# Batch 1's first transform in front of the fixed rows' read, and x laid out one tile to a transfer

## The chip, the core and the metric

The kernel runs on one core of a Trainium2 chip. The metric is device time in microseconds from start to end of one execution on that core; lower is better. Five engines work side by side, each through its own list of instructions in order: TensorE (PE, with its weight loads as PEld), VectorE (DVE), ScalarE (ACT), GpSimd (POOL) and SyncE (SP). All but TensorE and VectorE also issue transfers (DMAs) here, and these run on 16 DMA engines.

## The reference

A spectral filter over each of 8 batches, and behind it a mixture of 8 experts in which each row goes to one expert only.

```python
batch, seq, dim = (8, 2496, 256)            # float32
X = np.fft.rfft(x, axis=1)
F = (filt_r + 1j * filt_i)[None, :, :]
y = np.fft.irfft(X * F, n=seq, axis=1)      # -> 19968 rows of 256

xn = y / (norm(y) + 1e-06);  en = expert_emb / (norm(expert_emb) + 1e-06)
logits = xn @ en.T / tau
expert_idx = np.argmax(logits, axis=1)
gate_w = softmax(logits)[arange, expert_idx]
for e in range(8):                          # w1[e]: 256 x 1024, w2[e]: 1024 x 256
    mask = expert_idx == e
    h = np.maximum(y[mask] @ w1[e], 0.0)
    out[mask] = gate_w[mask, None] * (h @ w2[e])
```

## The kernel before, in words

**The transform.** 2496 = 64 × 39, so each batch's transform is done as matrix products: a first one over 39 points (`conv_s1`, tiles s_g_t: 11 tiles of 117 x 2 rows of x for batch g), a second one over 64 points with the filter in its middle (`conv_s2`, 10 steps of s and sa), and an inverse over 39 (`conv_sb`, tiles y). Between the stages the rows are written to DRAM (SD, ZD) and read back in another order (tiles a, and f for both the filter and ZD). Tiles of x are read into four buffers called `in`, which the tiles a share.

**The experts.** Rows of y get a norm, logits and the routing (`route`, L705), in chunks: batch 0 is routed as 12 and 10 half tiles. GpSimd then scatters each half tile to its expert's region of a table in DRAM (XS, `scatter_rows` L794). Work on the experts is cut into slots. A slot reads 128 or 256 rows of one expert back, transposed (`read_pair` L892, `read_rows` L882; tiles xTf and metaf for batch 0), multiplies with the expert's first matrix in four parts (ph_j_0 to ph_j_3, L973), takes the relu on ScalarE and VectorE (h_j_p, L981 and L982) and multiplies with the second matrix (po, L998). The first eight slots, one for each expert, are of 128 rows each and need only the first chunk of batch 0's rows. They are called the fixed rows here.

**The weights.** Each expert's matrices come as float32 (L264) and are made into a scaled float16 high half (ScalarE, L324) and a low half (VectorE, L331). Their scale comes from a product of the matrix with itself (gram, 16 small products, L286), its diagonal's greatest value (dg and wmax, L291 and L292) and a sum of that (L296).

**The order.** In the head, 82 steps long, the order on TensorE, VectorE, ScalarE and SyncE is that of the code (L1166 to L1177). In each step `head()` issues one piece of the transforms, `weights(n)` what is due of the weights, and from step 66 (SLOTS) a part of a slot follows. From step 35 on `head()` walks through batch 0's inverse (`back`, with its routing) and through batch 1's first transform (`ahead`) side by side: step n of `back` is head step 35 + n.

```python
        for n, w in enumerate(back):
            if n == XNEXT - 35:
                next(ahead)
            ...
            yield w
            if n >= SIDE and n not in PAUSE:
                next(ahead, 0)
        yield from ahead
```

At XNEXT the first x tiles of batch 1 are asked for. From step SIDE of `back` one of its 11 tiles is transformed in each step, save in the steps of PAUSE. Of `weights(n)`, WLOADS says in which steps the 16 halves of the weights are loaded, WPREP what of their preparation is done in a step (g: product, d: diagonal, p and q: scale, k: high half, l: low half, each with expert and part), and at step FIRST_ROWS = 64 the first two experts' fixed rows are read. WLATE does the rest of the preparation, by the count of slot parts.

Transfers issued by SyncE and ScalarE count up one of eight counters, DMAHW0 to DMAHW7, which are given to them in turn; a transfer waits until the one before it on its counter has landed.

Behind the head the order is worked out by a scheduler, from costs that are the same in both kernels.

Of the kernel before, what the change touches and what calls it, by code (L numbers as in the profile page):

```python
# [13 lines left out]
F32 = mybir.dt.float32  # L14
# [10 lines left out]
P = 128  # L25
NA, NB39 = 64, 39
S = NA * NB39
NK2 = 20
A3 = 3
TOK = A3 * NB39  # L30
NAG = (NA + A3 - 1) // A3
D = 256
# [8 lines left out]
XYB, INB, CYB = 6, 4, 7  # L41
# [4 lines left out]
G_S1, G_SB, G_S2, G_SA = 2, 3, 4, 3  # L46
DLAG = 2
MID = 8
XNEXT = 45
WLOADS = (38, 40, 42, 44, 46, 48, 50, 52, 54, 56, 58, 60, 62, 64, 78, 79)  # L50
WPREP = {43: "g00", 44: "g01", 46: "d0", 47: "p0", 48: "q0", 49: "k00 g10", 50: "l00 k01", 51: "l01 k02 g11",
# [5 lines left out]
WLATE = {16: "l53 q6 g70", 17: "k60 g71", 18: "l60 k61 d7", 19: "l61 k62 p7", 20: "l62 k63 q7", 21: "l63 k70",  # L57
         22: "l70 k71", 23: "l71 k72", 24: "l72 k73", 25: "l73"}
SIDE, PAUSE = 24, (28, 29, 30)
CLEAR, FIRST_ROWS = 39, 64  # L60
SLOTS, HEAD = 66, 82
WARM = {-1: 8, 12: 26, 35: 22, 40: 6}
# [12 lines left out]
def moe_spectral_kernel(  # L75
# [287 lines left out]
    def widths(g):  # L363

        return NAG * GROUPS[g][0] // 2, NK2 * GROUPS[g][0] // 2


    def whole(g, ap, t, rows, full):

        if GROUPS[g][0] == 2:  # L370
            k = rows(t)
            return [(slice(0, 2), k, ap(t, k, False))]
        if rows(2 * t) == rows(2 * t + 1):
            return [(slice(0, 2), full, ap(t, full, False))]
        return [(slice(j, j + 1), rows(2 * t + j), ap(2 * t + j, rows(2 * t + j), True)) for j in range(2)]

    def x_at(g):
        def at(t, k, half):
            if GROUPS[g][0] == 2:
                return x[first[g]:first[g] + 2, t * TOK:t * TOK + k].rearrange("b p c -> p b c")  # L380
            if half:
                return x[first[g], t * TOK:t * TOK + k].unsqueeze(1)
            return x[first[g], t * 2 * TOK:(t + 1) * 2 * TOK].rearrange("(j p) c -> p j c", j=2)
        return at

    def buf_at(g, buf):
        def at(t, k, half):
            if GROUPS[g][0] == 2:
# [9 lines left out]
    def load(q, g, pool, tag, t, ap, rows, full):  # L398
        it = pool.tile([P, 2, D], F32, tag=tag, name=f"{tag}{g}_{t}")
        got = []  # L400
        for h, k, m in whole(g, ap, t, rows, full):
            q.dma_start(it[:k, h], m)  # L402
            got.append((h, it[:k, h].rearrange("p j c -> p (j c)")))
        return got

    cons = {"c1": c1_sb, "c2": c2_sb, "m1": m1_sb, "csb": csb_sb}

# [41 lines left out]
    def conv_s1(g):  # L449

        NTL, _ = widths(g)
        if g == G_S1:
            cons["c1"] = parts_of(cons["c1"], "c1")
        xin = {t: load(nc.gpsimd if g > 1 else nc.sync, g, cin, "in", t, x_at(g), tokens, TOK) for t in range(INB - 1)}
        if g == 1:
            yield 0
        for t in range(NTL):
            if t + INB - 1 < NTL:
                xin[t + INB - 1] = load(nc.gpsimd if g > 1 else nc.sync, g, cin, "in", t + INB - 1, x_at(g), tokens, TOK)
            if g >= G_S1:  # L460
                u = t
                xin[u] = split(*pair(f"xp{g}_{u}"), xin[u])
            pool, tag = (ps_h, "h") if g == 1 and t < 4 else (ps_c, "c")
            pt = pool.tile([P, 2, D], F32, tag=tag, name=f"s1_{g}_{t}")
            for h, xt in xin.pop(t):
                product(pt[:, h].rearrange("p j c -> p (j c)"), cons["c1"], xt)
            st = cst.tile([P, 2, D], F32, tag="st", name=f"s{g}_{t}")
            nc.scalar.copy(st, pt)  # L468
            for h, k, m in whole(g, buf_at(g, SD[g]), t, freqs, 120):
                (nc.scalar if g == 1 else nc.sync).dma_start(m, st[:k, h])  # L470
            yield W_S1
# [233 lines left out]
    def route(g, out_rows, t0, n, rows, ssq, rr, lp, sg=None):  # L705
# [39 lines left out]
        oh = big("oh", F16)  # L745
        v.tensor_tensor(out=oh, in0=w8.unsqueeze(1).to_broadcast([P, nt, E]), in1=bc(mv), op=ALU.is_equal)
        yield 1
        if not g and t0 + n // 2 < widths(g)[0]:
            yield 1

        nc.scalar.activation(ex, l, AF.Exp)
        state["routed"] += 1
        base = state["base"]
# [310 lines left out]
    def head():  # L1064
        yield from conv_s1(0)
        yield from conv_s2(0)
        back, ahead = conv_sb(0), conv_s1(1)
# [3 lines that stand above are left out]
            if state["routed"] and not run["fixed"]:  # L1071
                run["fixed"] = True
                enqueue(0, "fixed")
            yield w
            if n >= SIDE and n not in PAUSE:
                next(ahead, 0)
        yield from ahead

# [177 lines left out]
```

## Time and profile before

| | before |
|---|---|
| median of 3 runs | 1359.09 us (1356.71, 1364.03, 1359.09) |
| the profiled execution | 1363.88 us, of it 1361.6 in the span |
| mean granted clock of TensorE | 0.963 |
| TensorE busy | 1246.3 us (92%), weight loads 980.6 (72%) |
| VectorE, ScalarE, GpSimd busy | 69%, 56%, 38% |
| moved by DMA | 240.64 MB |
| loads of x (L402) | 60 of 234 KB each on GpSimd and 20 on SyncE, with the two halves of the last tile beside them |

The profile is of one execution. A window's row gives each engine's busy time in a stretch, with its count of instructions. A row of the timeline gives the start, the duration, the engine, the line, the operation with output and inputs, and in brackets the idle time just ahead with what ended it. SPq, ACTq and POOLq are transfers being issued by SyncE, ScalarE and GpSimd. PEclk is the clock that TensorE was granted, as a share of full speed.

### The profile page before, as it was taken

Reading aid. Unit: us, or ns where it says so; the run is one execution under the profiler, and the core shown is the slowest. Engines: PE = TensorE matmul, PEld = TensorE weight load, DVE = VectorE, ACT = ScalarE, POOL = GpSimd, SP = SyncE. Lnnn points to the kernel's source line nnn. Section 1 sums busy time; section 2 is a strip of 40 time slices with the busy share of each in tenths; the row PEclk is TensorE's granted clock in tenths of the full one; section 3 lists DMA queues with packets and bytes.
Section 4 is the critical chain, followed back from the end, with each engine's and each line's share of the span. In section 5 each row is a group of like instructions: output and inputs, shape, how many; then the busy total and the mean of one; then the engine's idle time right before and its main releaser. Section 6 shows DMA issues by size and latency. Waiting matters only on the chain.

```text
span 1361.6 us, 36510 instructions
## 1 busy us (share of the span) xinstructions
PE 1246.3 (92%) x11027; PEld 980.6 (72%) x11027; DVE 940.1 (69%) x3078; ACT 761.5 (56%) x1760; POOL 513.2 (38%) x575
## 2 busy tenths in 40 slices
PE   7865799959997989999999999999999999999998
PEld 2333575635665768777788788878887788889887
DVE  1456686765676758887879787878786786444664
ACT  2174545744673668567747794768465843333343
POOL 0004413174337424752365347443642165211212
PEclk9987899979998989999999999999999899999999
DMA  7898787877987677777778797878774544231221
GB/s 225 270 324 282 207 246 205 187 218 229 198 176 214 195 185 176 199 226 178 174 181 242 185 200 184 228 188 195 169 201 139 129 119 106 52 60 40 48 48 41
DMA packets 275758, 240.64 MB, mean 177 GB/s; under 512 B 167845, under 2 KB 217902, under 8 KB 273777
## 3 DMA queue, kind: packets, MB, share of 16 engines
q1 hardware_dynamic: 246409, 177.71, 51.4%
q0 software_dynamic: 25280, 57.51, 14.5%
q10 hardware_dynamic: 3880, 3.03, 0.7%
q8 instruction: 104, 1.70, 0.6%
q14 instruction: 85, 0.70, 0.2%
HBM read 121.68 MB, written 85.57 MB: 152 GB/s over the span
## 4 chain that ended last, share of the span: by engine, by line
PE 64%; DMA 13%; issue 5%; DVE 4%; ACT 3%; POOL 1%; SPq 0%; DVEq 0%; POOLq 0%; ACTq 0%
PE ph L973 25%; PE po L998 24%; PE s L447 4%; DMA yT<-rows 4%; PE y L447 3%; DMA a<-SD 2%; PE sa L447 2%; PE s L442 2%; DMA f<-ZD 2%; DMA XS<-rows,ixi 1%; PE y L442 1%; PE tp L596 1%; PE lp L613 1%; DVE wp L957 1%; DMA SD<-s 1%
## 5 line engine op out<-in xcount | busy, mean ns | idle before, releaser
L998 PE MATMUL po<-W,h 128*128 (+1 forms) x3824 | 494.3, 273 | 0.0
L973 PE MATMUL ph<-xT,wp 128*128 128x256 f16 (+2 forms) x4224 | 476.2, 260 | 11.0 <-DMA xT<-XS 5.2
L973 PEld LDWEIGHTS <-wp 128*128 128x128 f16 x4224 | 360.6, 99 | 90.2 <-issue 40.5
L998 PEld LDWEIGHTS <-h 128*128 128x128 f16 x3824 | 361.2, 98 | 70.2 <-issue 27.6
L981 ACT ACTIVATE h<-ph 128x512 f16<-128x512 f32 (+2 forms) x384 | 202.0, 528 | 249.0 <-PE ph L973 194.7
L1013 POOL DMA_INDIRECT out_dram<-o,meta x153 | 159.4, 1042 | 309.8 <-ACT o L1012 231.0
L982 DVE SCALAR_TENSOR_TENSOR h<-ph,h 128x512 f16<-128x512 f32 (+2 forms) x384 | 227.3, 592 | 57.3 <-ACT h L981 55.4
L957 DVE COPY wp<-W 128x1024 f16 x352 | 168.0, 478 | 113.1 <-PE ph L973 108.5
L796 POOL DMA_INDIRECT XS<-rows,ixi x176 | 185.3, 1053 | 126.3 <-issue 53.7
L539 POOL TENSOR_TENSOR yy<-yy,xs 128x512 f32<-128x512 f32 x60 | 80.8, 1350 | 107.5 <-DVE xs L502 74.8
L402 POOL DMA_DIRECT2D in<-in_x x72 | 56.4, 784 | 161.2 <-DVE xp L416 44.2
L500 DVE TENSOR_TENSOR yy<-s,f 128x256 f32<-128x256 f32 x160 | 61.4, 418 | 63.6 <-ACT xs L532 25.8
L671 ACT ACTIVATE rows<-y 128x256 f16<-128x256 f32 x176 | 67.3, 398 | 35.1 <-PE y L442 33.3
L638 DVE SCALAR_TENSOR_TENSOR rows<-y,rr,rows 128x256 f16<-128x256 f32 x176 | 76.6, 477 | 14.7 <-ACT rows L635 13.4
L1012 ACT ACTIVATE o<-po,meta 128x256 f32<-128x256 f32 x148 | 64.2, 480 | 27.8 <-PE po L998 27.5
L635 ACT ACTIVATE rows<-y,rr 128x256 f16<-128x256 f32 x176 | 75.7, 499 | 6.3 <-DVE rr L676 5.1
L561 ACT COPY z<-sa 128x512 f32<-128x512 f32 x80 | 46.8, 585 | 50.0 <-PE sa L558 43.7
L468 ACT COPY s<-s 128x512 f32<-128x512 f32 x88 | 52.7, 600 | 30.8 <-PE s L442 14.5
L415 ACT CAST yp<-yy 128x512 fp32r<-128x512 f32 x50 | 30.9, 619 | 62.5 <-POOL yy L539 62.3
L598 ACT COPY yT<-tp 128x512 f16<-128x512 f16 x99 | 59.0, 610 | 7.0 <-PE tp L596 5.9
L447 PE MATMUL s<-xp,c1h 117*128 117x512 f32 (+1 forms) x144 | 60.8, 429 | 0.6 <-DVE sg L217 0.6
L613 PEld LDWEIGHTS <-yT 128*128 128x128 f16 x704 | 32.7, 97 | 37.2 <-DMA yT<-rows 18.2
(208 smaller groups left out, 1679.5 us busy)
## 6 DMA issues: line engine op xcount, KB each, us to landing
f<-in_filt SPq DMA_DIRECT2D x160, 256.0 KB
a<-SD SPq DMA_DIRECT2D x80, 256.0 KB
ZD<-z SPq DMA_DIRECT2D x80, 256.0 KB
f<-ZD SPq DMA_DIRECT2D x80, 240.0 KB
SD<-s SPq DMA_DIRECT2D x70, 240.0 KB
W<-in_w SPq DMA_DIRECT2D x14, 1024.0 KB
in<-in_x POOLq DMA_DIRECT2D x60, 234.0 KB
in<-in_x SPq DMA_DIRECT2D x20, 234.0 KB
```

The source lines that it names most:

```text
L447: nc.tensor.matmul(out_, w[:k], b, start=(n == 0), stop=(n == 2))
L539: nc.gpsimd.tensor_tensor(out=yy, in0=yy, in1=xs, op=ALU.add)
L635: nc.scalar.activation(rows[:, i, 0:D], y[:, i], AF.Copy, scale=rr[:, u:u + 1])
L638: nc.vector.scalar_tensor_tensor(out=rows[:, i, D:2 * D], in0=y[:, i], scalar=rr[:, u:u + 1], in1=rows[:, i, 0:D], op0=ALU.mult, op1=ALU.s ...
L671: nc.scalar.activation(rows[:, i, D:2 * D], y[:, i], AF.Square, accum_out=ssq[:, u + i:u + i + 1])
L796: i = nc.gpsimd.indirect_dma_start(out=XS, out_offset=bass.IndirectOffsetOnAxis(ap=ix, axis=0), in_=src, in_offset=None)
L957: last["dve"] = nc.vector.tensor_copy(wp, src)
L973: last["pe"] = nc.tensor.matmul(ph[:, fi, :size], wp[:, k * 2 + wh, fi * P:(fi + 1) * P], xT[:, xh * 2 + k, :size], start=(c == 0), stop=( ...
L981: last["act"] = nc.scalar.activation(h[:, 0, :, :size], ph[:, :, :size], AF.Relu)
L982: last["lo"] = nc.vector.scalar_tensor_tensor(out=h[:, 1, :, :size], in0=ph[:, :, :size], scalar=0.0, in1=h[:, 0, :, :size], op0=ALU.max, ...
L998: nc.tensor.matmul(self.po[:, s], h, self.Wp[:, off + wh * 1024:off + wh * 1024 + D], start=(fp == 0 and fi == 0 and c == 0), stop=(fp == ...
L1013: i = nc.gpsimd.indirect_dma_start(out=out, out_offset=bass.IndirectOffsetOnAxis(ap=self.meta[:n, s, 0:1].bitcast(I32), axis=0), in_=o, in ...
```

## The change

It does three things.

1. The x tiles of batch 1 are asked for two steps sooner (XNEXT 45 to 43), and the transform of them starts at step 18 of `back` instead of 24 and is not paused: head steps 53 to 63, in place of 59 to 62 and 66 to 72. All of it stands ahead of FIRST_ROWS = 64. In `route`, one of the two pauses behind the first chunk's `oh` goes.
2. The last two weight loads of the first run come a step sooner, and WPREP and WLATE are laid out anew: most pieces one to three steps later, the last at count 27 in place of 25.
3. x is laid out on the way in as 8 × 11 × 117 × 2 × 256, padded with zeros, so that a tile is one transfer in which each partition gets one run of 2048 bytes. Before, a tile was two runs of 1024 bytes per partition, and the last one, of 117 and 39 rows, came in two transfers. Now it is full, too.

```diff
@@ -46,17 +46,17 @@
 G_S1, G_SB, G_S2, G_SA = 2, 3, 4, 3
 DLAG = 2
 MID = 8
-XNEXT = 45
-WLOADS = (38, 40, 42, 44, 46, 48, 50, 52, 54, 56, 58, 60, 62, 64, 78, 79)
-WPREP = {43: "g00", 44: "g01", 46: "d0", 47: "p0", 48: "q0", 49: "k00 g10", 50: "l00 k01", 51: "l01 k02 g11",
...
-WLATE = {16: "l53 q6 g70", 17: "k60 g71", 18: "l60 k61 d7", 19: "l61 k62 p7", 20: "l62 k63 q7", 21: "l63 k70",
...
-SIDE, PAUSE = 24, (28, 29, 30)
+XNEXT = 43
+WLOADS = (38, 40, 42, 44, 46, 48, 50, 52, 54, 56, 58, 60, 61, 63, 78, 79)
+WPREP = {43: "g00", 44: "g01", 46: "d0", 48: "p0", 49: "q0 g10", 50: "k00", 51: "l00 k01 g11", 52: "d1 l01 k02",
...
+WLATE = {16: "l52 k53 p6", 17: "l53 q6 g70", 18: "k60 g71", 19: "d7 l60 k61", 20: "l61 k62", 21: "l62 k63 p7",
...
+SIDE = 18
 CLEAR, FIRST_ROWS = 39, 64
 SLOTS, HEAD = 66, 82
 WARM = {-1: 8, 12: 26, 35: 22, 40: 6}
@@ -374,15 +374,6 @@
             return [(slice(0, 2), full, ap(t, full, False))]
         return [(slice(j, j + 1), rows(2 * t + j), ap(2 * t + j, rows(2 * t + j), True)) for j in range(2)]
 
-    def x_at(g):
-        def at(t, k, half):
-            if GROUPS[g][0] == 2:
-                return x[first[g]:first[g] + 2, t * TOK:t * TOK + k].rearrange("b p c -> p b c")
-            if half:
-                return x[first[g], t * TOK:t * TOK + k].unsqueeze(1)
-            return x[first[g], t * 2 * TOK:(t + 1) * 2 * TOK].rearrange("(j p) c -> p j c", j=2)
-        return at
-
     def buf_at(g, buf):
         def at(t, k, half):
             if GROUPS[g][0] == 2:
@@ -402,6 +393,12 @@
             q.dma_start(it[:k, h], m)
             got.append((h, it[:k, h].rearrange("p j c -> p (j c)")))
         return got
+
+    def load_x(g, t):
+
+        it = cin.tile([P, 2, D], F32, tag="in", name=f"in{g}_{t}")
+        (nc.gpsimd if g > 1 else nc.sync).dma_start(it[:TOK], x[first[g], t])
+        return [(h, it[:k, h].rearrange("p j c -> p (j c)")) for h, k, _ in whole(g, lambda *a: None, t, tokens, TOK)]
 
     cons = {"c1": c1_sb, "c2": c2_sb, "m1": m1_sb, "csb": csb_sb}
 
@@ -451,12 +448,12 @@
         NTL, _ = widths(g)
         if g == G_S1:
             cons["c1"] = parts_of(cons["c1"], "c1")
-        xin = {t: load(nc.gpsimd if g > 1 else nc.sync, g, cin, "in", t, x_at(g), tokens, TOK) for t in range(INB - 1)}
+        xin = {t: load_x(g, t) for t in range(INB - 1)}
         if g == 1:
             yield 0
         for t in range(NTL):
             if t + INB - 1 < NTL:
-                xin[t + INB - 1] = load(nc.gpsimd if g > 1 else nc.sync, g, cin, "in", t + INB - 1, x_at(g), tokens, TOK)
+                xin[t + INB - 1] = load_x(g, t + INB - 1)
             if g >= G_S1:
                 u = t
                 xin[u] = split(*pair(f"xp{g}_{u}"), xin[u])
@@ -745,9 +742,6 @@
         oh = big("oh", F16)
         v.tensor_tensor(out=oh, in0=w8.unsqueeze(1).to_broadcast([P, nt, E]), in1=bc(mv), op=ALU.is_equal)
         yield 1
-        if not g and t0 + n // 2 < widths(g)[0]:
-            yield 1
-
         nc.scalar.activation(ex, l, AF.Exp)
         state["routed"] += 1
         base = state["base"]
@@ -1072,7 +1066,7 @@
                 run["fixed"] = True
                 enqueue(0, "fixed")
             yield w
-            if n >= SIDE and n not in PAUSE:
+            if n >= SIDE:
                 next(ahead, 0)
         yield from ahead
 
@@ -1227,8 +1221,10 @@
     fr = filt_r[src.T].transpose(0, 1, 2)
     fi = filt_i[src.T].transpose(0, 1, 2)
     filt = np.stack([np.concatenate([fr, fr], 1), np.concatenate([fi, fi], 1)], 2)
+    xp = np.zeros((nb, 2 * ((NAG + 1) // 2) * TOK, D), x.dtype)
+    xp[:, :S] = x[:, perm]
     arrays = {
-        "x": x[:, perm],
+        "x": xp.reshape(nb, -1, 2, TOK, D).transpose(0, 1, 3, 2, 4),
         "filt": filt,
         "sgn": sgn,
         "c1": c1,
```

SyncE around the fixed rows' first read. `in_k` is the tile k of x, W half an expert's matrices, XS the table of rows, SD what the first transform writes. Before:

```order
L264 DMA W<-in_w 128x2048 [waits DMAHW0_49]
L402 DMA in_6_1325<-in_x 117x2x256 [waits DMAHW2_49,PE_49]
L884 DMA_TRANSPOSE xTf_1350<-XS 128x4x128 [waits DMAHW3_49,DMASW3_49]
L885 DMA metaf_1351<-XS 128x2 [waits DMAHW4_49]
L884 DMA_TRANSPOSE xTf_1350<-XS 128x4x128 [waits DMAHW5_49]
L885 DMA metaf_1354<-XS 128x2 [waits DMAHW7_49]
L264 DMA W<-in_w 128x2048 [waits DMAHW0_49]
L402 DMA in_7_1418<-in_x 117x2x256 [waits DMAHW1_49,PE_49]
L884 DMA_TRANSPOSE xTf_1460<-XS 128x4x128 [waits DMAHW2_49]
L885 DMA metaf_1461<-XS 128x2 [waits DMAHW4_49]
```

Now:

```order
L264 DMA W<-in_w 128x2048 [waits DMAHW6_49]
L400 DMA in_10_1286<-in_x 117x512 [waits DMAHW0_49,PE_49]
L264 DMA W<-in_w 128x2048 [waits DMAHW1_49]
L264 DMA W<-in_w 128x2048 [waits DMAHW3_49]
L878 DMA_TRANSPOSE xTf_1393<-XS 128x4x128 [waits DMAHW4_49,DMASW3_49]
L879 DMA metaf_1394<-XS 128x2 [waits DMAHW5_49]
L878 DMA_TRANSPOSE xTf_1393<-XS 128x4x128 [waits DMAHW7_49]
L879 DMA metaf_1397<-XS 128x2 [waits DMAHW0_49]
L878 DMA_TRANSPOSE xTf_1477<-XS 128x4x128 [waits DMAHW1_49]
L879 DMA metaf_1478<-XS 128x2 [waits DMAHW3_49]
```

Before, the reads of the first two experts' rows have a load of W and of in_7 between them, and in_8 to in_10 come later still. Now all of x and three loads of W stand ahead, and the four reads follow each other. The third read is given DMAHW1 and the columns behind it DMAHW3.

ScalarE at the same place: s_k are tiles of batch 1's first transform, ex_6 and ixi_6 belong to the routing of batch 0's second chunk, h_0_0 to the first fixed slot. Before:

```order
L468 COPY s_3_1329<-s_1_3_1327 128x512 [waits PE_49]
L470 DMA SD_209<-s_3_1329 120x2x256 [waits DMAHW3_49,Activation_49]
L751 ACTIVATE ex_6_1344<-l_6_1332 128x80 [waits DVE_49]
L776 CAST ixi_6_1387<-ix_6_1385 128x10 [waits DVE_49]
L324 ACTIVATE W<-W,wsc 128x1024 [waits DMAHW2_49]
L324 ACTIVATE W<-W,wsc 128x1024
L981 ACTIVATE h_0_0_1415<-ph_0_0_1402 128x2x128 [waits PE_49]
```

Now:

```order
L465 COPY s_9_1364<-s_1_9_1362 128x512 [waits PE_49]
L467 DMA SD_209<-s_9_1364 120x2x256 [waits DMAHW6_49,Activation_49]
L465 COPY s_10_1378<-s_1_10_1375 128x512 [waits PE_49]
L467 DMA SD_209<-s_10_1378 120x256 [waits DMAHW1_49,Activation_49]
L467 DMA SD_209<-s_10_1378 40x256 [waits DMAHW3_49]
L745 ACTIVATE ex_6_1387<-l_6_1367 128x80 [waits DVE_49]
L770 CAST ixi_6_1432<-ix_6_1430 128x10 [waits DVE_49]
L324 ACTIVATE W<-W,wsc 128x1024
L975 ACTIVATE h_0_0_1455<-ph_0_0_1442 128x2x128 [waits PE_49]
```

Before, s_3 is written out ahead of ex_6, and s_4 follows behind h_0_0. Now s_9 and s_10 stand there. The first write of s_10 waits on DMAHW1, the second on DMAHW3; both are given their counter behind the reads.

TensorE where batch 1's second transform (s_1_0) begins; gram and ph belong to the weights and the slots. Before:

```order
L286 LDWEIGHTS wraw_3_1915
L286 MATMUL gram_2054<-wraw_3_1915 128x128
L442 MATMUL s_1_0_2133<-a_0_2085,c_sb 128x512
L442 MATMUL s_1_1_2158<-a_1_2087,c_sb 128x512
L296 LDWEIGHTS one_142
L296 MATMUL gram_1823<-wmax,one_142 128x2
L973 LDWEIGHTS W
L973 MATMUL ph_3_3_1978<-xTf_1460,W 128x128
```

Now:

```order
L286 LDWEIGHTS W
L286 MATMUL gram_1495<-W 128x128
L439 MATMUL s_1_0_2114<-a_0_2059,c_sb 128x512
L439 MATMUL s_1_1_2139<-a_1_2061,c_sb 128x512
L967 LDWEIGHTS W
L967 MATMUL ph_0_3_1556<-xTf_1393,W 128x128
```

Before, s_1_0 stands ahead of ph_3_3, the last part of the fourth slot. Now it stands ahead of ph_0_3, the last part of the first one.

## Rows read from the trace of the kernel before

**Rows 1.** Windows: busy times by stage, granted clock and DMA share.

```profile
core 0: us, PE busy (x) PEld busy (x) DVE busy (x) ACT busy (x) POOL busy (x), PEclk, DMA share, GB/s
97.80:131.90 34.10, 22.19 (x186) 14.64 (x187) 23.55 (x82) 18.30 (x39) 15.23 (x13) 0.70 0.90 303
131.90:140.90 9.00, 0.04 (x2) 0.04 (x2) 2.93 (x16) 1.47 (x4) 0.17 (x1) 0.50 0.56 159
140.90:148.10 7.20, 7.20 (x65) 5.41 (x65) 4.17 (x11) 3.03 (x6) 5.72 (x5) 0.71 1.18 291
148.10:227.70 79.60, 74.47 (x686) 53.14 (x684) 60.12 (x159) 44.78 (x78) 18.50 (x18) 1.00 0.71 215
...
238.30:312.90 74.60, 55.88 (x488) 37.05 (x489) 49.10 (x248) 42.80 (x124) 33.66 (x41) 0.84 0.79 204
```

**Rows 2.** Waits of TensorE, 0 to 260: total, times, longest.

```profile
PE gram L296 <- DVE wmax L292: 14.8, 4, 9.0
...
PE s L442 <- DMA in<-in_x: 4.9, 5, 1.8
```

**Rows 3.** Timeline of TensorE around the hole.

```profile
140.86 0.16 PE L296 MATMUL gram<-wmax,one 128*128 128x2 bf16 x1 [8.97 <-DVE wmax L292]
140.88 1.44 PE L973 MATMUL ph<-xTf,W 128*128 128x128 f16 x12
...
146.08 1.08 PE L442 MATMUL s<-in,c_sb 117*128 117x512 f32 x2
146.99 1.08 PE L286 MATMUL gram<-W 128*128 128x128 bf16 x16
147.91 0.83 PE L973 MATMUL ph<-xTf,W 128*128 128x128 f16 x12
```

**Rows 4.** Timeline of the other engines, routing and first read.

```profile
112.11 1.88 POOL L796 DMA_INDIRECT XS<-rows,ixi  x1 [19.47 <-DVE done L878]
...
128.80 1.79 POOL L796 DMA_INDIRECT XS<-rows,ixi  x1 [0.30 <-issue]
...
134.11 1.31 SPq L884 DMA_TRANSPOSE xTf<-XS  x1
...
136.92 0.32 ACTq L470 DMA_DIRECT2D SD<-s  x1
137.29 0.27 ACT L751 ACTIVATE ex<-l 128x80 f32<-128x80 f32 x1 [8.48 <-DMA xTf<-XS]
...
137.59 0.24 DVE L763 TENSOR_REDUCE se<-ex 128x10 f32<-128x80 f32 x1 [6.38 <-ACT ex L751]
...
139.70 0.20 ACT L776 CAST ixi<-ix 128x10 int32<-128x10 f32 x1 [2.14 <-DVE ix L773]
...
142.77 0.42 DVE L982 SCALAR_TENSOR_TENSOR h<-ph,h 128x256 f16<-128x256 f32 x1 [0.51 <-ACT h L981]
142.86 3.04 SPq L489 DMA_DIRECT2D f<-in_filt  x4
```

**Rows 5.** Chain that ended last: start, length, step.

```profile
128.80 5.30 DMA XS<-rows,ixi
134.11 2.74 DMA xTf<-XS
...
172.84 7.39 DMA a<-SD
...
197.86 2.44 DMA a<-SD
```

**Rows 6.** DMA queue at 12 to 16, then 30 to 35.

```profile
q1 hardware_dynamic: 1169, 1.13, 90.4%
...
q1 hardware_dynamic: 842, 1.54, 94.0%
```

**Rows 7.** Timeline of TensorE, batch 1's first inverse row.

```profile
238.25 2.07 PE L442 MATMUL y<-f,csb_sb 120*128 120x512 f32 x2 [3.39 <-DMA f<-ZD]
```

**Rows 8.** Costly lines 0 to 260: the low halves on VectorE.

```profile
L331 DVE SCALAR_TENSOR_TENSOR W<-W,wsc 128x1024 f16<-128x1024 f32 x27 | 34.3, 1274 | 3.7 <-ACT W L324 3.7
```

More of the change, by code (lines that the diff above doesn't have):

```diff
@@ L48 @@
 MID = 8
-XNEXT = 45
-WLOADS = (38, 40, 42, 44, 46, 48, 50, 52, 54, 56, 58, 60, 62, 64, 78, 79)
-WPREP = {43: "g00", 44: "g01", 46: "d0", 47: "p0", 48: "q0", 49: "k00 g10", 50: "l00 k01", 51: "l01 k02 g11",
[5 rows of a table removed]
-WLATE = {16: "l53 q6 g70", 17: "k60 g71", 18: "l60 k61 d7", 19: "l61 k62 p7", 20: "l62 k63 q7", 21: "l63 k70",
-         22: "l70 k71", 23: "l71 k72", 24: "l72 k73", 25: "l73"}
-SIDE, PAUSE = 24, (28, 29, 30)
+XNEXT = 43
+WLOADS = (38, 40, 42, 44, 46, 48, 50, 52, 54, 56, 58, 60, 61, 63, 78, 79)
+WPREP = {43: "g00", 44: "g01", 46: "d0", 48: "p0", 49: "q0 g10", 50: "k00", 51: "l00 k01 g11", 52: "d1 l01 k02",
[5 rows of a table added]
+WLATE = {16: "l52 k53 p6", 17: "l53 q6 g70", 18: "k60 g71", 19: "d7 l60 k61", 20: "l61 k62", 21: "l62 k63 p7",
+         22: "l63 q7", 23: "k70", 24: "l70 k71", 25: "l71 k72", 26: "l72 k73", 27: "l73"}
+SIDE = 18
 CLEAR, FIRST_ROWS = 39, 64
```

10 rows, old and new, of the table WPREP are left out of this document.

## The prediction

> **What bounds the kernel now.** I read the profile from the front to the place where the two orders become alike again: first the windows, then TensorE's waits, the timeline around the widest hole, the chain that ended last, and the DMA queue. The windows [rows 1] show where TensorE has room: 22.19 busy of 34.1 us while batch 0 is routed (97.8 to 131.9), 0.04 of 9.0 just behind it (131.9 to 140.9), then 74.47 of 79.6 (94%) up to the end of batch 1's middle stages, and 55.88 of 74.6 in the stage where batch 1 is routed. Behind 312.9 TensorE is 92 to 100% busy by the page's slices, so a lead won before then reaches the end unless a wait swallows it. The stage from 238 to 312.9 is such a candidate: routing, scatters and the read follow each other there. But its order on TensorE is the same in both kernels from batch 1's first inverse row [rows 7], so I take it as a fixed length behind that row. The question is how much sooner the row at 238.25 comes.
>
> The largest single wait is 9.0 us for a norm of the weights on VectorE, L292 [rows 2]. The timeline [rows 3, 4] shows that the norm is only the last of a chain. The last scatter of the first chunk is issued at 128.80, takes 5.30 to land [rows 5], and at 134.11 SyncE issues the first transposing read, which lands 2.74 later, 136.85. ScalarE's write of s_3 is issued at 136.92, and `ex` behind it on ScalarE starts at 137.29: both had waited for the read, since that write waits for the counter (DMAHW3) that the read counts up. Then VectorE's seven small steps (137.59 to 139.70), the norm, and at 140.86 TensorE runs again.
>
> **The change part by part.**
> *First transform moved in front of the read.* Seven tiles of x come to stand in front of the hole. A tile takes 0.91 us on TensorE at full clock (146.08 to 146.99 [rows 3]), 6.4 in all; the room in 97.8 to 131.9 is 11.9 us [rows 1], so they hide there if x is there in time. Two of the seven stood between ph_0_0 and ph_0_2 before, five behind ph_0_2. What follows ph_0_2 at 147.91 is a full stretch, so there the five save 5 × 0.91 = 4.55. A norm's product (16 matmuls, 146.99 to 147.91: 0.92) goes in front too. About 0.5 of slot work moves the other way, behind the second transform (an estimate: half a product of the kind at 147.91). Net 4.1 us less between ph_0_2 and the end of the second transform.
>
> *The start of that stretch.* The read is the fixed point; call its issue T. T follows the last scatter. The pause of one step that is taken out of the routing lets the scatters begin sooner than 112.11 [rows 4], but 4 x tiles, one W and all the SD writes now share the DMA queues with them. If the scatters, 1.5 us apart on average now ((128.80 − 112.11)/11), came back to back at about 1.3, T would be near 131.5; if the traffic pushes them, up to 142 (below). I take 133.6, half a microsecond sooner, near the row of 134.11.
> The new wait: on ScalarE the two writes of s_10 now wait for DMAHW1 and DMAHW3, and these are the counters of the third transposing read and of its meta columns; `ex`, `ixi`, a W piece and h_0_0 stand behind them. The four reads took from 134.11 to 142.86 less about 0.9 for the W and x issues between them, 7.85 in all [rows 4], so the third is issued at about T + 4.0, lands 2.74 later, its meta near T + 7.8. From there as in the trace: `ex` 0.3, VectorE's chain 2.1 (137.59 to 139.70), `ixi` 0.2, then to the end of h_0_0's VectorE half 2.4 (139.90 to 143.19 is 3.3 now, with two W pieces in it; one remains). That is T + 12.8; ph_0_2 follows at about T + 13.5, or 147.1 to 147.5. Before it was 147.91. Lead here 0.6; the bounds are 2.6 (T at 131.5) and −7.5 (T at 142).
>
> *A second idle stretch.* Now TensorE stops twice: before ph_0_0, and from the end of the first products to ph_0_2, about 8 us, because nothing is left to lay between. Behind the hole of 9 us the granted clock was 0.71 over 7.2 us [rows 1], and the same product took 1.44 and later 0.83 us [rows 3]. That cost 7.2 × 0.29 = 2.1 us. I book it once more: −2.1; its bounds are 0 (the clock holds) and −2.1.
> The Trainium skill, "TensorE: Matmul & The Clock Gate", section "Part 1: The HAM clock gate", says that the engine has two rates and falls to the lower one after idling; the rows agree (0.50 of full speed in the hole, which is 1.2 of 2.4 GHz, and 0.71 behind it). It speaks against this change, as filler that stood between waits is taken out of them; without it the sum below would be 2.1 better.
>
> *The second transform's reads.* a_0 is issued behind the four reads and four f (3.04): T + 10.9, and lands 2.44 to 7.39 later [rows 5]; it is needed about T + 16, behind ph_0_2, its down product and a norm. With the usual 4 it is there; with 7.39 TensorE waits 2.3.
>
> *W pieces.* Two more low halves at 1.27 [rows 8] stand behind h_0_0 on VectorE, 19 instead of 17. VectorE's 60.12 of 79.6 (75%) becomes some 64.4 of 75.5 (85%). It hides under TensorE's 94%, and I cost it at nothing; uncovered it is 2.5 us.
>
> *Layout of x.* Runs of 2048 bytes instead of 1024. Between 12 and 16 us, mostly such reads and writes, 1169 packets of 967 bytes took 90.4% of 16 engines × 4 us, 49.5 ns each, 51 ns per 1000 bytes; between 30 and 35, mostly of 2 KB, 842 packets took 89 ns for 1829 bytes, 49 ns per 1000 [rows 6]. That is 5% of a tile, 0.04 us each, and the last tile grows by 80 KB, 0.25 us. So the transfer itself brings nothing. TensorE waits for x 4.9 us in all, five times [rows 2]; between 0 and 4.9 can go, and by the near row of the packets it is close to the lower end: 0.3. GpSimd issues six fewer loads of 0.8 us; GpSimd is 38% busy: 0.
>
> **The sum.** 0.6 + 4.1 − 2.1 + 0.3 = 2.9 us sooner. Against the profiled execution (span 1361.6, 1363.88 with the 2.3 around it) that is 1361.0. That execution lies 4.8 above the median of the runs shown, 1359.09, so against the median it is 1356.
>
> **The rivals.**
> *A, the whole hole is won.* The writes of s_10 are issued before the reads' counters come round, or wait for little; `ex` runs beside the first read, and ph_0_2 comes at about T + 9. Then the second idle stretch is gone with its clock: 4.1 + 0.6 + 4.5 + 0.3 = 9.5, 1350. For it: the routing is a step sooner. Against it: on ScalarE the writes of s_10 stand ahead of `ex` by the order, and before, one such write did wait for a read (136.92).
> *B, VectorE becomes the bound: slower.* h_0_0 ends near T + 12.8 = 146.4 where it ended at 143.19, and behind it VectorE has two more low halves. If W's low halves then arrive after TensorE wants them, the late 3.2 and 2.5 go to the path, with the second clock loss 2.1: 7.8 later, 1367. It decides when VectorE's busy share from 147 to the end of the second transform passes some 85%. Against it: 10% stays free even so.
> *C, the DMA engines are the bound ahead of the read.* 3.9 MB (one W of 1.05, four x tiles, eight SD writes) come in front of T at 303 GB/s, 13 us of traffic, and the share in 97.8 to 131.9 is 0.90, which leaves 3.4 us of that stretch; up to 8 us of it pushes T back. Then 2.9 − 8 is 5 us slower, but half of that is given back as the traffic is missing behind the read: 1361 to 1364. The Trainium skill, "DMA: Bandwidth & Descriptors", section "Issuing engines are not separate DMA queues", says that transfers issued by several engines interleave on the same 16 hardware engines; by that the writes from ScalarE and scatters from GpSimd share these 16, and it gives C its chance.
> *D, the change does little:* what is moved is won ahead of 238 and waited for behind it, at the scatters: 1359.
>
> **How the numbers follow.** The forecast 0.44; A 0.30, B 0.14, C 0.07, D 0.05. This kernel's measurement tells a difference from none at about 0.5%, 6.8 us: faster is below 1352.3, slower above 1365.9. Forecast, C and D fall within, save for some 0.04 that the forecast goes further (T at 131.5, clock held) and 0.02 of C; so faster 0.34, same 0.50, slower 0.16. The range reaches from A with 3 us more (1347) to B (1367); the forecast's own is 1350 to 1362 (T, the clock and the last x wait at their ends).
>
> **What would show it.** Right: one hole before ph_0_0 and a second of about 8 us behind it, with a clock below 0.8 behind each; `ex` of the last chunk starting after the third read has landed; the first inverse row of batch 1 near 235.5 instead of 238.25; x waits near 4.6 us. Wrong: `ex` beside the first read (A), T past 138 (C), waits of TensorE for L331 between 150 and 230 (B), or a first inverse row much sooner with the same end (D).

## The result, and the profile after

The changed kernel takes 1347.26 us, the median of 14 runs (1340.07 to 1355.43), the kernel before 1357.68 beside it (1351.47 to 1365.66): ratio 0.9918, 95% interval [0.9898, 0.9938]. That is 10 to 11 us sooner, where 2.9 were forecast and no measurable change held to be likeliest.

| | before | after |
|---|---|---|
| profiled execution, span | 1363.88, 1361.6 | 1344.95, 1343.2 |
| TensorE busy | 1246.3 | 1246.3 |
| first read issued (T) | 134.11 | 130.53 |
| ph_0_2 | 147.91 | 146.07 |
| batch 1's first inverse row | 238.25 | 225.89 |
| first full slot of batch 1 | 312.89 | 299.26 |

The two profiled executions lie 19 us apart, since that of before lies near the top of its runs and that of after in the lower half. The rest behind the first full slot takes 1048.7 and 1043.9 us. In six profiles on chips of this speed, of both kernels and of versions of them, it takes 1038 to 1049, whichever the kernel: the ends of single profiles tell nothing below 10 us, the stages do. So the stages are read here, and the ends from the medians.

The windows of the changed kernel, in the stages of [rows 1] (the last ends with its first full slot):

```profile
core 0: us, PE busy (x) PEld busy (x) DVE busy (x) ACT busy (x) POOL busy (x), PEclk, DMA share, GB/s
95.85:130.53 34.68, 26.78 (x159) 14.96 (x159) 21.51 (x76) 19.88 (x43) 13.08 (x14) 0.71 1.01 354
130.53:141.03 10.50, 4.21 (x32) 2.53 (x33) 3.64 (x13) 4.13 (x7) 0.00 (x0) 0.95 1.07 301
141.03:146.07 5.04, 4.86 (x52) 4.79 (x52) 3.52 (x18) 2.29 (x4) 0.99 (x1) 0.50 0.90 267
146.07:225.89 79.82, 77.86 (x760) 58.43 (x759) 68.58 (x179) 47.23 (x86) 24.47 (x27) 1.00 0.71 210
225.89:299.26 73.37, 55.31 (x488) 36.98 (x488) 48.44 (x248) 43.07 (x124) 32.30 (x43) 0.86 0.86 211
```

TensorE in the changed kernel, from the last x tiles to the second transform, then the first inverse row:

```profile
133.48 2.13 PE L439 MATMUL s<-in,c_sb 117*128 117x512 f32 x6
141.03 0.23 PE L753 MATMUL rk<-oh,lt 128*128 128x80 f16 x1 [5.43 <-DVE oh L743]
...
141.82 0.16 PE L296 MATMUL gram<-wmax,one 128*128 128x2 bf16 x1 [0.18 <-DVE wmax L292]
141.85 2.72 PE L967 MATMUL ph<-xTf,W 128*128 128x128 f16 x24
144.36 1.91 PE L286 MATMUL gram<-W 128*128 128x128 bf16 x16
146.07 1.17 PE L967 MATMUL ph<-xTf,W 128*128 128x128 f16 x12
...
148.66 1.93 PE L439 MATMUL s<-a,c_sb 128*128 128x512 f32 x4
```

```profile
225.89 1.12 PE L439 MATMUL y<-f,csb_sb 120*128 120x512 f32 x2 [1.41 <-DMA f<-ZD]
```

To be seen: one hole of 5.43 us, in front of `rk`, and behind it an unbroken row up to ph_0_2. The clock is 0.50 for 5.04 us behind the hole and full from ph_0_2 on; so the loss of a low clock was paid once, 2.5 us, as it was before (2.1). There is no second idle stretch. x is worked off at 135.6, and s_1_0 begins at 148.66 without a wait.

What the hole waits for, on the other engines:

```profile
123.15 0.98 POOL L790 DMA_INDIRECT XS<-rows,ixi  x1 [0.30 <-issue]
...
130.53 1.34 SPq L878 DMA_TRANSPOSE xTf<-XS  x1
...
136.65 0.32 ACTq L467 DMA_DIRECT2D SD<-s  x1
...
137.02 1.15 ACT L324 ACTIVATE W<-W,wsc 128x1024 f16<-128x1024 f32 x1 [3.88 <-DMA SD<-s]
...
138.20 1.28 DVE L331 SCALAR_TENSOR_TENSOR W<-W,wsc 128x1024 f16<-128x1024 f32 x1 [4.47 <-ACT W L324]
...
139.41 0.23 DVE L732 TENSOR_REDUCE mx<-l 128x10 f32<-128x80 f32 x1
```

```profile
139.65 0.73 ACTq L467 DMA_DIRECT2D SD<-s  x2
...
140.49 0.27 ACT L745 ACTIVATE ex<-l 128x80 f32<-128x80 f32 x1 [0.87 <-DVE mv L737]
...
140.74 0.24 DVE L743 TENSOR_TENSOR oh<-w,mv 128x80 f16<-128x80 f32 x1
...
144.28 5.80 SPq L479 DMA_DIRECT2D a<-SD  x5
```

And one step of the chain that ended last (start, length, step):

```profile
125.71 10.87 DMA SD<-s
```

The read is issued 3.6 us sooner than at [rows 4], with 354 GB/s in the window ahead of it. The last scatter is issued 5.7 us sooner (123.15 against 128.80), but the read follows it by 7.4 us, where it was 5.3. ScalarE's write of s_8 goes out at 136.65 only, when an earlier write of s has landed: that one had been issued at 125.71 and took 10.87 us. A W piece behind the write of s_8 waited 3.88 us, VectorE's low half waits for the W piece, and `mx`, the next step of the routing, stands behind the low half. So `oh` comes at 140.74, and TensorE stands at `rk`. The two writes of s_10, which the prediction has waiting for the third read and its columns, are issued at 139.65 as soon as ScalarE gets to them.

From ph_0_2 to the first inverse row it was 90.34 us and is 79.82. First the window of this stretch before and TensorE's waits in it, then the waits after:

```profile
147.91:238.25 90.34, 81.83 (x757) 58.74 (x754) 64.65 (x168) 49.59 (x88) 22.97 (x26) 0.99 0.74 216
```

```profile
PE gram L296 <- DVE wmax L292: 2.5, 2, 1.4
PE s L442 <- issue: 1.2, 1, 1.2
PE gram L286 <- DMA wraw<-in_w: 0.6, 1, 0.6
PE s L442 <- DMA in<-in_x: 0.6, 1, 0.6
```

```profile
PE ph L967 <- DVE h L976: 0.5, 1, 0.5
```

TensorE's work there fell from 81.83 to 77.86, by 4.0; its idle time from 8.51 to 1.96, by 6.5. Of these, norms' sums held 2.5, a stop with no wait shown 1.2, W and x 1.2, and the row of 3.39 at [rows 7] is 1.41 now. VectorE is 86% busy there (68.58 of 79.82) and holds TensorE for 0.5 us.

### The profile page after: what moved, and what is told of

It is laid out like the page before. It is cut to its first block, busy times and chain, and to the rows that moved or that the text cites. A ratio compares the mean times of both kernels' runs of the same rounds, so it can differ in the third digit from the quotient of the medians.

```text
span 1343.2 us, 36499 instructions
## 1 busy us (share of the span) xinstructions
PE 1246.3 (93%) x11027; PEld 981.2 (73%) x11027; DVE 938.8 (70%) x3078; ACT 762.2 (57%) x1760; POOL 489.2 (36%) x569
## 4 chain that ended last, share of the span: by engine, by line
PE 71%; DMA 18%; DVE 4%; issue 3%; ACT 2%; POOL 1%; SPq 1%; ACTq 0%; DVEq 0%; POOLq 0%
PE ph L967 27%; PE po L992 26%; PE s L444 5%; DMA yT<-rows 4%; DMA f<-ZD 3%; PE sa L444 3%; PE y L444 2%; DMA f<-in_filt 2%; DMA W<-in_w 2%; PE s L439 2%; PE sa L555 2%; DMA XS<-rows,ixi 1%; DMA SD<-s 1%; PE y L439 1%; PE lp L610 1%
## 5 line engine op out<-in xcount | busy, mean ns | idle before, releaser
L967 PE MATMUL ph<-xT,wp 128*128 128x256 f16 (+2 forms) x4224 | 471.6, 258 | 10.9 <-DMA xT<-XS 3.7
L951 DVE COPY wp<-W 128x1024 f16 x352 | 164.8, 469 | 117.8 <-PE ph L967 115.3
L790 POOL DMA_INDIRECT XS<-rows,ixi x176 | 180.1, 1023 | 142.0 <-issue 93.8
L400 POOL DMA_DIRECT2D in<-in_x x66 | 38.8, 588 | 168.8 <-DVE xp L413 57.3
```

Source lines behind the costliest of these rows:

```text
L790: i = nc.gpsimd.indirect_dma_start(out=XS, out_offset=bass.IndirectOffsetOnAxis(ap=ix, axis=0), in_=src, in_offset=None)
L951: last["dve"] = nc.vector.tensor_copy(wp, src)
L967: last["pe"] = nc.tensor.matmul(ph[:, fi, :size], wp[:, k * 2 + wh, fi * P:(fi + 1) * P], xT[:, xh * 2 + k, :size], start=(c == 0), stop=( ...
```

## The experiments

There were six sets, each on another chip, with the kernel before run in turn in the same set. In one set (set 2) the kernel before takes 1358.2 us, as in the first measurement; in the others 1478 to 1488, so those chips are 9% slower with every kernel. The changed kernel itself ran in sets 2 and 6 only. Set 2 is taken first.

### Set 2 (before: 1358.2): the change and its parts

**r_changed**, the changed kernel again. 

> The changed kernel once more, beside the experiments. Where the kernel before takes about 1357 us: ratio 0.990 to 0.994, as first measured. Where it takes about 1483 us, as in the set of e1 to e5, with TensorE standing still without a wait between 500 and 1200 us: theory P (those pauses give a lead back) says 0.998 to 1.002; the rival, that a lead is kept whatever the chip does behind it, says 0.990 to 0.994.

Measured: 1346.35, ratio 0.9923 [0.9893, 0.9953]. The profile has the same shape:

```profile
144.66 0.23 PE L753 MATMUL rk<-oh,lt 128*128 128x80 f16 x1 [4.70 <-DVE oh L743]
...
149.43 0.83 PE L967 MATMUL ph<-xTf,W 128*128 128x128 f16 x12
```

```profile
229.29 1.12 PE L439 MATMUL y<-f,csb_sb 120*128 120x512 f32 x2 [1.16 <-DMA f<-ZD]
```

ph_0_2 is 1.5 us later than at [rows 3] here, and the stretch up to the first inverse row takes 79.86 us, within 0.1 of the first profile. The first full slot comes at 299.20. The chain is the same, too: the write of s that s_8's waits for takes 12.0 us to land here, and the read follows the last scatter by 6.9 us. So the start swings by some 3 us between the two executions, while the shortening of this stretch stands.

**r_layout_only**, in the kernel before only the loads of x:

```diff
-        xin = {t: load(..., "in", t, x_at(g), tokens, TOK) for t in range(INB - 1)}
+        xin = {t: load_x(g, t) for t in range(INB - 1)}
```

> The kernel before with x in the new layout alone, again, for a set in which the changed kernel runs beside it. Theory O (order makes the gain): 0.998 to 1.001. Theory L (layout makes it): 0.995 or less, or about the ratio of the changed kernel.

Measured: 1352.61, 0.9963 [0.9931, 0.9995]. In its profile ph_0_2 is at 148.39 and the first inverse row at 237.46, 0.8 sooner than before, the stretch between them 89.1. On another chip (**e1_layout_only**, before 1483.4) it was 0.9994 [0.9964, 1.0024]. 

> The kernel before with x in the new layout alone. Theory O (the gain comes from the order of the first transform): at the front about 1.9 us at most, as between the two traces at batch 0's inverse (97.80 against 95.85), so a ratio of 0.998 to 1.001 to before. Theory L (the layout makes the gain): 0.995 or less.

The two together: between nothing and half a per cent. Set 2's ratio lies between the ranges of theories O and L. Its trace shows 0.8 us up to the inverse row and 3.8 at the first full slot of batch 1 (309.10), and the trace of e1_layout_only has no such lead there (322.96, against 321.17 in before_diag_in_place below).

**r_order_only**, the changed kernel with the old loads of x (the edit above the other way round). 

> The changed kernel with x in its old layout, again. Theory O: within 0.2% of the changed kernel in this set. Theory L: within 0.2% of the kernel before.

Measured: 1344.96 over only 5 runs, 0.9889 [0.9836, 0.9943]: the order alone has the whole gain, as theory O has it. But its profiled execution does not show it in the same place:

```profile
142.51 0.22 PE L756 MATMUL rk<-oh,lt 128*128 128x80 f16 x1 [2.78 <-DVE oh L746]
...
150.55 0.83 PE L970 MATMUL ph<-xTf,W 128*128 128x128 f16 x12 [1.79 <-DVE h L979]
...
154.82 3.61 PE L442 MATMUL s<-a,c_sb 128*128 128x512 f32 x4 [1.86 <-DMA a<-SD]
```

```profile
146.12 0.27 ACT L748 ACTIVATE ex<-l 128x80 f32<-128x80 f32 x1 [2.43 <-DMA SD<-s]
```

The hole before `rk` is 2.78 us, then TensorE waits for h_0_0 and for a_0, as `ex` on ScalarE stood 2.43 us behind the second write of s_10. With one transfer more in the old layout, the counters fall otherwise, and this write has that of the fourth read, not of the third's columns. The first inverse row is at 235.46, and the rest behind the first full slot is the shortest of all, 1038.1. The row is 2.8 us sooner than before and the first full slot (308.11) 4.8. Time and profile don't agree on where the gain lies; the five runs say that it is there.

**r_writes_off_scalar**, the changed kernel with three of ScalarE's writes on GpSimd:

```diff
-                (nc.scalar if g == 1 else nc.sync).dma_start(m, st[:k, h])
+                ((nc.gpsimd if t >= 8 else nc.scalar) if g == 1 else nc.sync).dma_start(m, st[:k, h])
```

> The changed kernel with the writes of s_8 to s_10 issued by GpSimd, again. Theory W (ScalarE's wait on the counters costs): 0.2 to 0.4% below the changed kernel in this set, hole before ph_0_0 2 us or less. Rival D (the DMA engines are the bound there): within 0.2% of the changed kernel.

Measured: 1349.66, 0.9925 [0.9894, 0.9956], no different from the changed kernel. On TensorE, and VectorE's step that it waits for:

```profile
138.67 0.20 PE L753 MATMUL rk<-oh,lt 128*128 128x80 f16 x1 [1.45 <-DVE oh L743]
...
142.45 0.16 PE L296 MATMUL gram<-wmax,one 128*128 128x2 bf16 x1 [3.32 <-DVE wmax L292]
```

```profile
141.52 0.42 DVE L291 TENSOR_TENSOR dg<-gram,ident 128x256 f32<-128x256 f32 x1 [2.90 <-DMA SD<-s]
```

`rk` waits 1.45 instead of 5.43, as theory W has it. But 3.32 come back at the norm's sum: dg writes into one of three buffers that it shares with the tiles s, and that buffer is free only when a write of s has landed. ph_0_2 comes at T + 14.2. Most of the wait was moved, not removed, and the time is within 0.2% of the changed kernel, as rival D has it. (**e4_writes_off_scalar**, the same on the chip of set 1: 1.0007 [0.9981, 1.0033].) 

> The changed kernel, but the writes of s_8, s_9 and s_10 are issued by GpSimd, so ScalarE does not stand behind the counters of the reads and W loads. Theory W (that wait holds the routing's last steps on VectorE and so the hole of 5.4 us on TensorE): the hole falls to 2 us or less, ph_0_2 comes about 3 us sooner than 146.07 and the ratio to before is 0.987 to 0.990. Rival D (the DMA engines, 99% busy from 105 to 145, are the bound there): the hole shrinks but the second transform waits for a_0 as much longer; ratio 0.991 to 0.994 as the changed kernel.

### Both things that hold the hole (set 4, before 1486.6)

dg writes over the gram in PSUM:

```diff
-            dg = cst.tile([P, 2, P], F32, tag="st", name=f"dg{e}")
+            dg = gram[e][:, :, :P]
```

**diag_and_writes**, with GpSimd's writes as above. 

> The changed kernel with dg in place and the writes of s_8 to s_10 issued by GpSimd: both things that held the routing's last steps and the norm are gone. With GpSimd's writes alone the hole was 1.45 us ahead of rk and 3.3 ahead of the norm's sum, where dg waited for a write of s. Theory W+B: hole 2 us or less in all, ph_0_2 3 to 5 us sooner after the read's issue, ratio to before 0.987 to 0.990. Rival D (the DMA engines bound the stage): a_0 is waited for instead, 0.991 to 0.994.

```profile
144.16 0.20 PE L753 MATMUL rk<-oh,lt 128*128 128x80 f16 x1 [1.45 <-DVE oh L743]
...
144.96 0.16 PE L296 MATMUL gram<-wmax,one 128*128 128x2 bf16 x1 [0.35 <-DVE wmax L292]
146.39 2.72 PE L967 MATMUL ph<-xTf,W 128*128 128x128 f16 x24 [1.27 <-DMA xTf<-XS]
...
155.47 1.12 PE L439 MATMUL s<-a,c_sb 128*128 128x512 f32 x2 [1.67 <-DMA a<-SD]
```

Measured: 1.0001 [0.9966, 1.0035]. `rk` waits 1.45, the norm's sum 0.35; now ph_0_0 waits 1.27 for the read itself, and the second transform 1.67 for its a. ph_0_2 is at T + 15.8, where the changed kernel on such a chip has it at T + 19.4 (changed_again, below): 3.6 us sooner, and the first inverse row is at 231.86 instead of 236.70. So for the stage W+B holds, save that the transfers are now waited for. But the first full slot comes at 323.65 instead of 317.10, and the ratio fits neither W+B nor rival D.

**diag_in_place**, dg's edit alone in the changed kernel. 

> The changed kernel with the diagonal product dg written over the gram in PSUM instead of into one of the three buffers that the tiles s share, so dg waits for no write of s to land. Theory B (those buffers, held until SD writes have landed, cost the changed kernel little, since its x tiles are done by then): ratio to the changed kernel within 0.2%, so 0.991 to 0.994 to before; the hole before ph_0_0 stays near 5 us, as ScalarE still stands behind its writes.

 Measured: 1.0049 [1.0010, 1.0087], a little slower than before on this chip, where theory B had 0.991 to 0.994. I can't say why: the hole at `rk` is 5.92, and a norm's sum waits 3.23 us where no buffer can hold dg any more:

```profile
147.92 0.22 PE L753 MATMUL rk<-oh,lt 128*128 128x80 f16 x1 [5.92 <-DVE oh L743]
...
167.44 0.16 PE L296 MATMUL gram<-wmax,one 128*128 128x2 bf16 x1 [3.23 <-DVE wmax L292]
```

**before_diag_in_place**, dg's edit in the kernel before. 

> The kernel before with dg in place, all else as it was. Theory B (of the waits of 6.5 us between ph_0_2 and the first inverse row that the change took away, 2.5 stood ahead of norm sums because dg waited for a buffer of s): those two waits go, 2 to 3 us, ratio 0.997 to 0.999. Rival (they come from VectorE's queue): the two waits stay.

```profile
156.93 2.07 PE L442 MATMUL s<-in,c_sb 117*128 117x512 f32 x2 [3.85 <-ACT s L468]
...
173.44 0.16 PE L296 MATMUL gram<-wmax,one 128*128 128x2 bf16 x1 [1.15 <-DVE metaf L961]
```

Measured: 0.9998 [0.9960, 1.0037]. One of the two waits stays (1.15), and where the other was an x tile waits 3.85 us for ScalarE. So theory B explains one of the two waits at most, and the x tile's wait takes its place.

### W loads behind the reads (set 3, before 1477.9)

**w_behind_reads**, the changed kernel with two loads later:

```diff
-WLOADS = (..., 58, 60, 61, 63, 78, 79)
+WLOADS = (..., 58, 60, 70, 72, 78, 79)
```

> The changed kernel with the loads of W of steps 61 and 63 moved to steps 70 and 72, so that 2 MB leave the DMA queue ahead of the four reads and stand behind them, ahead of a_0. Theory D (the DMA engines, 99% busy ahead of the read, hold ScalarE's writes and with them the hole of 5 us): hole before ph_0_0 2 us or less, ph_0_0 3 to 6 us sooner than 141.9 to 145.5; but a_0 lands later, so 0.988 to 0.993. Rival W (the hole hangs on the counters shared with the reads, whatever the traffic): hole and time as in the changed kernel.

Measured: 0.9996 [0.9965, 1.0026].

```profile
142.20 0.20 PE L753 MATMUL rk<-oh,lt 128*128 128x80 f16 x1 [2.10 <-DVE oh L743]
...
145.11 3.22 ACTq L467 DMA_DIRECT2D SD<-s  x2
...
148.37 0.27 ACT L745 ACTIVATE ex<-l 128x80 f32<-128x80 f32 x1 [5.81 <-DMA W<-in_w]
...
152.80 1.44 PE L967 MATMUL ph<-xTf,W 128*128 128x128 f16 x12 [6.00 <-DVE h L976]
```

The hole at `rk` is 2.10 us, and the write of s_8 goes out at once (137.81, its copy ends at 137.64). Whether that is the smaller traffic or another deal of the counters, the run doesn't tell. ph_0_0 is at 143.02, but the writes of s_10 now have the counters of the two W loads: their issue takes 3.22 us, `ex` waits 5.81 for W to land, and ph_0_2 waits 6.00 for h_0_0. The wait went at one place and came back on ScalarE at another. Both theories have a part in it, and the ratio is outside of what either named.

### Parts of the order on the slower chips

**x_steps_only** in set 3, and three more runs of the same kernel, **e5_x_steps_only** (set 1), **x_steps_only_2** (set 4) and **x_steps_only_3** (set 5): before with XNEXT 43, SIDE 18 and no PAUSE.

```diff
-SIDE, PAUSE = 24, (28, 29, 30)
+SIDE, PAUSE = 18, ()
```

> The kernel before with the x tiles' steps alone (XNEXT 43, from step 18 on, no pause); the weights' tables, the routing's pause and the layout as before. Theory O (the gain is the x tiles' products taken out of the full stretch, and the waits that go with them): 0.990 to 0.994 to before, from ph_0_2 to the first inverse row of batch 1 about 80 us where it was 90.3. Rival T (the weights' pieces had to be laid out anew, too): 0.997 or more.

For e5_x_steps_only theory O stood at 0.992 to 0.996 and rival T at 0.998 to 1.004. For the last two runs 0.997 to 1.002 was expected on a slower chip. Measured in sets 1, 3, 4 and 5: 0.9981 [0.9947, 1.0016], 0.9998 [0.9960, 1.0035], 0.9980 [0.9942, 1.0019], 0.9989 [0.9945, 1.0034]. One of its profiles (x_steps_only_2):

```profile
140.49 0.23 PE L759 MATMUL rk<-oh,lt 128*128 128x80 f16 x1 [0.93 <-DVE oh L746]
...
144.76 0.16 PE L296 MATMUL gram<-wmax,one 128*128 128x2 bf16 x1 [3.66 <-DVE wmax L292]
...
159.26 1.10 PE L442 MATMUL s<-a,c_sb 128*128 128x512 f32 x2 [2.91 <-remote]
```

The norm's sum still waits 3.66 us there and the second transform 2.91, but the stretch from ph_0_2 (150.49) to the first inverse row (234.92) takes 84.4 us, and 84.1, 84.5 and 82.1 in the other three profiles. On such chips it is 93.2 with the layout alone and 92.4 with dg's edit alone, the two versions whose order is that of before, and 86.3 in the changed kernel (changed_again, below). So the tiles' steps by themselves shorten the stretch by as much as the whole change: for that, theory O holds. For the time it does not: 0.990 to 0.994 lies below all four intervals, each of which holds 1. The first two ratios lie in rival T's ranges, the last two where they were expected. The traces show where the lead goes. ph_0_2 comes at 150.5 to 154.4, where the two versions with the order of before have it at 150.1 and 148.1. From the first inverse row to the first full slot it then takes 82.5 to 84.8 us instead of 79.7 and 80.6. So the lead at the row, 2 to 8 us, is 0 to 4 at the first full slot. This kernel never ran on a chip of the first speed.

**pause_kept** (the changed kernel with the routing's pause) and **old_tables** (with WLOADS, WPREP and WLATE of before). 

> The changed kernel with the routing's pause of one step put back. Theory Y (the pause makes the scatters and the read sooner, 130.5 to 132.3 against 134.1): the read's issue 2 to 4 us later, the ratio to before 0.994 to 0.996. Theory O: the read may come later, but the hole takes it up, and the ratio stays 0.990 to 0.994.

> The changed kernel with the weights' tables (WLOADS, WPREP, WLATE) of before. Theory T: the high and low halves of before stand among the x tiles and hold ScalarE, VectorE and with them the routing; the ratio to before is 0.996 or more. Theory O: 0.990 to 0.994, the tables are worth 0.2% at most.

Measured: 0.9985 [0.9954, 1.0015] and 0.9993 [0.9958, 1.0027]. The read is issued at 137.76 with the pause, 132.37 with the old tables. ph_0_2 follows T by 9.6 and by 20.5 us: the later read finds ScalarE further on, and the old tables' W pieces hold it. Both ratios are above theory O's range. The old tables' lies in theory T's; the pause's lies above theory Y's, too. But the changed kernel did not run beside them.

**changed_again**, the changed kernel on such a chip (set 6, before 1488.2). 

> The changed kernel once more. Where the kernel before takes about 1480 us, theory P (pauses of TensorE behind the head give the lead back): 0.997 to 1.002, with batch 1's first inverse row still 4 us or more ahead of 240.5 to 243.3, where versions near the kernel before have it on such chips. Rival (the lead is kept on every chip): 0.990 to 0.994. Where the kernel before takes about 1357 us: 0.990 to 0.994 for both.

Measured: 1480.33, 0.9927 [0.9895, 0.9958]. In this set theory P is wrong: the change keeps its gain. Its lead does not show why: the first inverse row is at 236.70, among those of the x tiles' steps alone (234.9 to 238.4). And pause_kept has that row at 229.86 and diag_and_writes at 231.86, with ratios of 0.9985 and 1.0001. So on these chips the row does not set the time. What these chips do differently, in one window of 1040 us, r_changed first, then changed_again, and two of the latter's waits:

```profile
300.00:1340.00 1040.00, 1002.21 (x9209) 830.03 (x9207) 755.61 (x2419) 609.12 (x1411) 414.21 (x466) 0.99 0.63 159
```

```profile
300.00:1340.00 1040.00, 936.95 (x7610) 735.65 (x7609) 686.98 (x2240) 567.27 (x1302) 395.10 (x449) 0.93 0.62 158
```

```profile
PE ph L967 <- issue: 29.9, 43, 1.8
PE po L992 <- issue: 24.8, 37, 1.3
```

The granted clock is 0.93 instead of 0.99, TensorE gets through 7610 matmuls instead of 9209, and it stands still 72 us in the whole run for nothing that the profile shows, mostly 0.5 to 1.2 us at a time. Before changed_again I took it for the reason why the versions of sets 1 and 3 show no gain. It can't be the whole reason, as changed_again has these pauses and the gain, and nothing has taken its place: r_order_only's kernel has 0.9889 in set 2 and 1.0002 [0.9963, 1.0041] as **e2_order_only** in set 1, which the intervals don't reconcile. Whether it is the chip or the smaller edits' own is open. 

> The changed kernel with x in its old layout, so the new order alone. Theory O: 0.992 to 0.995 to before, the first inverse row of batch 1 at 226 to 228. Theory L: 0.998 or more, the row at 235 or later.

## Why the prediction was wrong, point by point

- **The work behind ph_0_2, 4.1 less.** Right: 4.0 (81.83 to 77.86).
- **The start, T = 133.6 and ph_0_2 at T + 13.5, lead 0.6.** T was 130.53 and 132.28, sooner than forecast, once sooner than my bound; ph_0_2 came T + 15.5 and T + 17.2, later. The two nearly cancel, by luck: leads of 1.8 and -1.5. The path behind T failed. I had the writes of s_10 wait for the third read (2.74 us to land) and its columns. They waited for neither. ScalarE stood at the write of s_8, two tiles earlier, behind an earlier write of s that took 10.87 us to land (12.0 in r_changed). That caught the routing a step sooner than I had it: `oh`, not `ex`.
- **A second idle stretch, -2.1.** This step failed. I had `rk` done before the hole, as it was before, and so ph_0_0 in front of `ex`. In the changed kernel `rk` itself stands behind the blocked VectorE, so the whole wait lies ahead of ph_0_0, and what follows runs through. One hole, 5.4 us where it was 9.0, and one low clock.
- **The rest of the stretch as it was, booked at nothing.** This is the larger miss: 6.5 us of waits went. I counted what the x tiles' products take and not what their neighbours wait for while these tiles share buffers, queues and ScalarE with the slots. 4.0 + 6.5 + 1.8 is the 12.4 at the first inverse row; in r_changed 4.1 + 6.4 - 1.5 is 9.0.
- **The second transform's a in time.** Right; issued at T + 13.8, not T + 10.9, and not waited for.
- **VectorE with more low halves, nothing.** Right at 86%: the bound of 85% in rival B was no bound.
- **x's layout, 0.3.** The waits for x went from 4.9 to 3.6 and 4.3 in the two profiles, of that order. The ratio of 0.9963 leaves room for more. Up to the inverse row no row shows it; behind it the one trace has 3 us, where I took the length as fixed.
- **Rivals.** A had the time (1350) and not the way: ph_0_2 came at T + 15.5, not T + 9. C's traffic came, with a DMA share of 1.01 at 354 GB/s ahead of the read. T was sooner all the same, as the scatters were issued 5.7 and 3.4 us sooner; but the read followed the last of them by 2.1 and 1.6 us more than before, and ScalarE's write took its 10.87 us to land in that traffic. The Trainium skill, "DMA: Bandwidth & Descriptors", section "Issuing engines are not separate DMA queues", says that transfers issued by ScalarE, SyncE and GpSimd run on the same 16 DMA engines and interleave. The trace is in keeping with it, with those 10.87 us at shares of 1.01 and 1.07 in the two windows. That the traffic is the cause is not shown.

By the traces it is the tiles' steps that shorten the stretch. That these alone bring the time is not shown, and on the slower chips four runs speak against it. On the faster ones the lead at the row (12.4 and 9.0 us) has the size of the gain, but r_order_only has the gain with a lead of 2.8 there. Which neighbour's wait each tile ends isn't shown either: dg's buffer was tried and explains one of two waits at most.

## What to carry to other kernels

When a step is moved out of a full stretch, price the waits that its neighbours have for its buffers and its engine's queue there, not its own duration alone. When a wait grows on one engine, follow each queue behind it up to the engine that bounds: which instruction stops first decides whether there is one hole or two. A transfer's counter can tie its issuer to an unrelated read or to an earlier write that is slow to land, and moving one transfer re-deals all of them. A lead seen at one row in the middle is not yet time: look for it again further on.

## What the runs showed of the hardware

The same kernel takes 1358 us on one chip and 1478 to 1488 on five others, with TensorE granted 0.96 to 0.97 and 0.92 to 0.94 of full speed over the span, and 2 to 4 and 65 to 77 us of pauses of TensorE with no wait that the profiles show. Executions of one kernel on one chip lie up to 20 us apart (1349.85 to 1369.24 for the kernel before in set 2). With DMA shares of 1.01 and 1.07 ahead of the read and behind it, a write of 240 KB took 10.87 us to land, and 12.0 and 10.5 in the other two profiles of the changed kernel.
